# One sync queue with 256 KB transfers, late loads per batch and spread out, and masks ahead of weight casts in a fused attention and feed-forward kernel

## The chip, the cores and the metric

The kernel runs on one core of one Trainium2 chip. The metric is the device time of one execution in microseconds (us); smaller is better. Besides the times there is one profiled execution of each kernel, with a trace of every instruction. The profile names the engines PE (TensorE matmuls), PEld (TensorE weight loads), DVE (VectorE), ACT (ScalarE), POOL (GpSimd) and SP (SyncE). SPq, ACTq and POOLq are the instruction queues from which an engine issues DMAs. "L383" is line 383 of that kernel's source.

## The reference

The first half is linear attention with a decay per head, in blocks along the sequence; the second half is a feed-forward layer with a sigmoid-approximated gelu. There are 4 batches, 8 heads, 768 tokens and a head dimension of 64; the feed-forward layer goes from 512 to 2048 and back.

```python
for b in range(nb):                       # blocks along the sequence (block = 64)
    qb, kb, vb = (q[:, :, sl], k[:, :, sl], v[:, :, sl])
    intra = einsum('bhic,bhjc->bhij', qb, kb) * Dmask     # causal mask with powers of lam
    intra = einsum('bhij,bhjd->bhid', intra, vb)
    inter = einsum('bhid,bhde->bhie', qb * lam_pow, kv_state)
    out[:, :, sl] = intra + inter
    kv_state = lam_block * kv_state + einsum('bhsd,bhse->bhde', kb_dec, vb)
x = out.transpose(0, 2, 1, 3).reshape(B * S, H * D)       # 3072 x 512
h = x @ w_in                                              # 512 -> 2048
g = h * (1 / (1 + exp(-1.702 * h)))
result = g @ w_out                                        # 2048 -> 512
```

## The kernel before

The 768 tokens of each batch are worked through in six "waves" (w = 0 to 5) of 512 columns. Waves 0 and 1 are made of small "units" (one batch and one pair of heads), for a quick start. Waves 2 to 5 are "full" waves of 128 tokens of all four batches. The feed-forward matmuls of wave w stand between the attention work of wave w + 1, so TensorE always has feed-forward work to do as long as the attention work next in its program is ready. TensorE takes its instructions in order. One that waits for data holds up everything behind it, as the wait of 4.75 us shown below does with the feed-forward matmuls that follow it.

All fp32 inputs land in a ring of SBUF buffers. A function per load is put on a list, and `pump()` issues the loads in order as the ring has room. Loads of late waves are put on that list by the schedule itself, at given points. In the kernel before, these late loads (w >= 3) are issued from GpSimd; all others are issued from SyncE:

```python
LATE = 3
...
def load_unit(w, nm, bl, p):              # one unit of one input: 128 KB
    def go(x):
        nc.sync.dma_start(
            out=x.rearrange("s (h c) -> s h c", h=2),
            in_=SRC[nm][2 * w + bl, 2 * p : 2 * p + 2, 0 : 2 * P, :].rearrange("h (q j) d -> q h (j d)", j=2))
        ...
def load_pair(w, nm, p):                  # a pair of heads of all batches: two DMAs of 128 KB
    def go(x):
        x = x.rearrange("s (b h d) -> s b h d", h=2, d=D)
        for h in range(2):
            (nc.sync if w < LATE else nc.gpsimd).dma_start(
                out=x[:, :, h, :],
                in_=SRC[nm][:, 2 * p + h, w * P : (w + 1) * P, :].rearrange("b s d -> s b d"))
        ...
```

A full wave casts and scales k and q on VectorE and then turns them around with a DMA transpose on SyncE's queue. The scores on TensorE need the transposed tile `kq`. The attention result is turned in the same way, from `xs` to `xT`, for the feed-forward layer:

```python
def p_cast(w, p):
    ...
    nc.sync.dma_start_transpose(out=kq_of[w, p].rearrange("p i b s -> p (i b) s"),
                                in_=kqs.rearrange("p i b h d -> p (i b h d)"))
def p_score(w, p):                        # TensorE, waits for kq
    ...
def p_out(w, p):
    ...
    nc.scalar.copy(xs.rearrange("s b h d -> s h b d"), o)
    nc.sync.dma_start_transpose(out=xT(w)[:, p], in_=xs.rearrange("p b h d -> p (b h d)"))
```

The start works through the eight units of wave 0 as a pipeline: unit i is cast and transposed on TensorE while unit i - 1 gets its scores and its state, and unit i - 2 its output:

```python
for i in range(N + 2):
    u, u1, u2 = ...                       # units i, i - 1, i - 2
    if u:
        fill(FILL1); u_turn(0, *u)        # TensorE transposes of the casts
    if u2:
        u_inter(0, *u2)
    if u:
        u_turn_copy(0, *u, nc.scalar)
    if u2:
        u_out(0, *u2)
    if i == N:
        for u_ in ROWS[:2]:
            cast_w("in", *u_, nc.vector)  # w_in casts, ahead of the last mask
    if u1:
        u_score(0, *u1); u_kv0(0, *u1)
        u_mask(0, *u1)                    # VectorE
        u_kv0_copy(0, *u1)                # two ScalarE instructions
    pump()
    ...
```

## Time and profile before

| what | before |
|---|---|
| time, median of 3 runs | 232.38 us (231.28 to 233.66) |
| the profiled execution | 239.61 us, span 237.9 us, mean granted clock 0.971 (a slow run) |
| TensorE busy | 214.9 us, 90% of the span |
| DMA queues | SyncE's 30.42 MB, GpSimd's 9.44 MB |

The profiled execution is some 7 us longer than the median, so sizes read from it must be scaled with care.

The page of the kernel before cuts the span into 40 slices (5.9 us each). A digit is the share of the slice in tenths that TensorE was busy, and that the TensorE clock was granted:

```profile
PE   7887998999999297999595999999999999999993
PEclk9997999999999679999999799999999999999999
```

TensorE is full except at the start and between slices 14 and 22 (some 77 to 130 us), and there the clock falls too. The table of busy time by window of the kernel before shows the middle closer. The columns are the window, its length, then busy time and (in brackets) number of instructions of PE, PEld, DVE, ACT and POOL, then the granted clock, the DMA share and GB/s:

```profile
60.00:72.00 12.00, 12.00 (x131) 6.91 (x128) 3.95 (x11) 7.19 (x19) 4.84 (x8) 1.00 1.18 232
72.00:84.00 12.00, 7.25 (x71) 5.12 (x69) 7.13 (x19) 4.04 (x11) 8.88 (x13) 0.79 1.03 158
84.00:96.00 12.00, 10.38 (x115) 5.31 (x113) 7.22 (x14) 1.17 (x2) 9.44 (x14) 0.92 1.13 193
108.00:130.00 22.00, 16.03 (x153) 8.10 (x152) 9.42 (x19) 8.39 (x15) 12.43 (x19) 1.00 1.12 152
130.00:170.00 40.00, 40.00 (x288) 19.00 (x286) 20.75 (x42) 13.07 (x22) 17.63 (x24) 0.96 0.70 153
```

What TensorE waited for is in the list of waits of the kernel before (total us, times, longest us):

```profile
PE ps_s L383 <- DMA kq<-kqs: 12.3, 5, 4.7
PE ps_o L358 <- DVE sm L301: 0.9, 1, 0.9
```

The scores (`ps_s`) wait 12.3 us for the DMA transposes. That transposes are slow here, and not late in the schedule, is in the view of the tile `kq`: its DMA line gives the issue time on SyncE's queue in ns (min/median/max), its last line the time to landing:

```profile
L374 SPq DMA_TRANSPOSE kq<-kqs x16: 1232/1358/4887, 73.1 to 181.6; - x16
DMA to landing us min/median/max: 3.1/6.1/15.1
```

By themselves (after 147 us) these transposes land in 3.1 to 3.8 us; between 73 and 130 us they take 8.5 to 15.1 us. In SyncE's timeline four of them occupy the queue for 13.79 us:

```profile
73.08 13.79 SPq L374 DMA_TRANSPOSE kq<-kqs  x4
```

TensorE's timeline of the kernel before shows what such a wait costs (start us, duration us, engine, line, operation, in brackets the idle time before it and its cause):

```profile
81.61 0.61 PE L383 MATMUL ps_s<-kq 64*128 64x128 bf16 x8 [4.75 <-DMA kq<-kqs]
82.15 0.61 PE L398 MATMUL ps_kv<-v_sb,kqs 128*128 128x128 bf16 x4
82.55 1.91 PE L470 MATMUL ps_out<-w_out,g_sb 128*128 128x512 bf16 x4
...
129.16 0.40 PE L383 MATMUL ps_s<-kq 64*128 64x128 bf16 x8 [2.53 <-DMA kq<-kqs]
130.07 4.44 PE L470 MATMUL ps_out<-w_out,g_sb 128*128 128x512 bf16 x12
```

The wait is paid twice. After 4.75 us of idle the four big matmuls take 1.91 us, where four take about 1.03 us at full clock; after 2.53 us of idle twelve take 4.44 instead of 2.75 us. After waits of 1.6 and 1.7 us, elsewhere in the same timeline, the clock stayed whole.

The same view of the start of the kernel before:

```profile
21.12 0.43 PE L358 MATMUL ps_o<-sm,v_sb 64*64 64x128 bf16 x8 [0.92 <-DVE sm L301]
21.48 3.56 PE L439 MATMUL ps_h<-xT,w_in 128*128 128x512 bf16 x9
```

A mask (`sm`) came 0.92 us late, because it stood behind a weight cast on VectorE, and the first nine feed-forward matmuls then ran at half clock.

### The profile page before, as it was taken

How to read it: one execution, taken by the hardware profiler on the slowest of the kernel's cores; microseconds unless marked ns; L12 is line 12 of the kernel's file. 1: busy time of each engine (PE TensorE's matmuls, PEld its weight loads, DVE VectorE, ACT ScalarE, POOL GpSimd, SP SyncE). 2: the span in 40 equal slices, each digit the busy share in tenths (PEclk: the TensorE clock that was granted, in tenths of full speed). 3: DMA queues.
4: the chain of work that ended last, by engine and by line, in shares of the span. 5: the costliest groups of instructions: out<-in, count | busy, mean ns of one | idle time of the engine just before them, and what ended most of it. 6: DMA issues, size and time to landing. Idle time of an engine off the chain costs nothing.

```text
span 237.9 us, 4615 instructions
## 1 busy us (share of the span) xinstructions
PE 214.9 (90%) x1772; PEld 109.5 (46%) x1772; DVE 106.8 (45%) x233; ACT 99.6 (42%) x211; POOL 81.8 (34%) x131
## 2 busy tenths in 40 slices
PE   7887998999999297999595999999999999999993
PEld 3453444665467144443253444454444454444453
DVE  3566455693238265555363228567153451200121
ACT  5795657655747000126340105661026630166100
POOL 7650051032339577598572996200000000000000
PEclk9997999999999679999999799999999999999999
DMA  5889989999999999999998999912329014110012
GB/s 143 248 209 350 362 227 329 363 257 218 229 230 204 120 195 196 225 247 172 180 138 149 199 229 272 163 25 47 112 88 176 15 32 133 46 44 0 35 56 88
DMA packets 63286, 40.16 MB, mean 169 GB/s; under 512 B 41376, under 2 KB 53920, under 8 KB 63264
## 3 DMA queue, kind: packets, MB, share of 16 engines
q1 hardware_dynamic: 59664, 30.42, 52.4%
q0 software_dynamic: 3456, 9.44, 21.2%
q8 instruction: 14, 0.23, 0.4%
q14 instruction: 8, 0.07, 0.1%
q10 hardware_dynamic: 144, 0.00, 0.0%
HBM read 27.27 MB, written 6.29 MB: 141 GB/s over the span
## 4 chain that ended last, share of the span: by engine, by line
PE 64%; DMA 27%; SPq 4%; ACT 1%; DVE 1%; issue 1%; POOL 0%; ACTq 0%
PE ps_out L470 30%; PE ps_h L439 24%; DMA kq<-kqs 13%; DMA xT<-xs 5%; DMA ring<-in_moe_w_in_dram 5%; SPq L90 4%; DMA ring<-in_q_dram 2%; PE ps_s L383 2%; PE ps_o L420 2%; DMA ring<-in_k_dram 2%; PE ps_out L486 1%; PE ps_t L275 1%; PE ps_kv L398 1%; PE ps_o L413 1%; PE ps_kv L336 1%; PE ps_s L296 1%
## 5 line engine op out<-in xcount | busy, mean ns | idle before, releaser
L439 PE MATMUL ps_h<-xT,w_in 128*128 128x512 bf16 (+1 forms) x448 | 89.6, 353 | 0.9 <-ACT g_sb L445 0.5
L470 PE MATMUL ps_out<-w_out,g_sb 128*128 128x512 bf16 x368 | 86.4, 390 | 0.0
L445 ACT ACTIVATE g_sb<-ps_h 128x512 bf16<-128x512 f32 (+1 forms) x112 | 59.6, 536 | 60.9 <-PE ps_h L439 59.5
L439 PEld LDWEIGHTS <-w_in 128*128 128x128 bf16 x448 | 42.6, 99 | 40.1 <-issue 3.6
L470 PEld LDWEIGHTS <-g_sb 128*128 128x128 bf16 x368 | 35.7, 100 | 41.1 <-issue 3.8
L390 DVE SCALAR_TENSOR_TENSOR sm<-ps_s,inv_pow,mask 128x512 bf16<-128x512 f32 x32 | 22.6, 747 | 37.1 <-PE ps_s L383 37.1
L477 DVE COPY o_sb<-ps_out 128x512 f32<-128x512 f32 x19 | 13.1, 691 | 54.3 <-PE ps_out L470 51.5
L423 ACT CAST xs<-ps_o 128x512 bf16<-128x512 f32 x16 | 9.4, 585 | 44.8 <-PE ps_o L420 29.2
L258 POOL TENSOR_TENSOR kqs<-ring,kq_pow 128x256 bf16<-128x256 f32 x16 | 10.2, 637 | 34.7 <-DMA ring<-in_q_dram 33.9
L101 POOL DMA_DIRECT2D ring<-in_q_dram x24 | 17.8, 747 | 5.6 <-DMA ring<-in_k_dram 4.5
L101 POOL DMA_DIRECT2D ring<-in_v_dram x24 | 17.9, 749 | 3.6 <-DMA ring<-in_q_dram 2.0
L101 POOL DMA_DIRECT2D ring<-in_k_dram x24 | 18.0, 756 | 0.7 <-DMA ring<-in_v_dram 0.6
L372 POOL CAST v_sb<-ring 128x512 bf16<-128x512 f32 x16 | 10.3, 662 | 23.0 <-DMA ring<-in_v_dram 20.3
L383 PE MATMUL ps_s<-kq 64*128 64x128 bf16 x128 | 6.6, 224 | 12.3 <-DMA kq<-kqs 12.3
L301 DVE TENSOR_TENSOR sm<-ps_s,mask 128x512 bf16<-128x512 f32 x16 | 11.0, 689 | 10.5 <-PE ps_s L296 6.1
L383 PEld LDWEIGHTS <-kq 64*128 64x128 bf16 x128 | 3.7, 96 | 19.6 <-DMA kq<-kqs 15.8
L370 DVE TENSOR_SCALAR kqs<-ring,k_pow 128x256 bf16<-128x256 f32 x32 | 11.7, 406 | 0.2
L370 DVE TENSOR_SCALAR kqs<-ring,q_pow 128x256 bf16<-128x256 f32 x32 | 11.8, 408 | 0.0
L402 DVE SCALAR_TENSOR_TENSOR kv<-kv,blk,ps_kv 64x256 bf16<-64x256 bf16 x24 | 11.4, 475 | 0.2
L258 DVE TENSOR_TENSOR kqs<-ring,kq_pow 128x256 bf16<-128x256 f32 x16 | 8.3, 529 | 5.2 <-ACT kq_pow L204 2.7
L250 PE MATMUL ps_f<-zeros 128*128 128x512 bf16 x28 | 8.7, 438 | 1.3 <-DVE zeros L173 1.3
L283 ACT COPY kq<-ps_t 128x512 bf16<-128x512 bf16 x12 | 7.0, 585 | 5.8 <-PE ps_t L275 5.4
(66 smaller groups left out, 135.2 us busy)
## 6 DMA issues: line engine op xcount, KB each, us to landing
ring<-in_moe_w_in_dram SPq DMA_DIRECT2D x16, 256.0 KB, 6.5
ring<-in_moe_w_out_dram SPq DMA_DIRECT2D x16, 256.0 KB, 5.3
out_dram<-o_sb SPq DMA_DIRECT2D x15, 256.0 KB, 2.2
ring<-in_k_dram SPq DMA_DIRECT2D x24, 128.0 KB, 3.6
ring<-in_q_dram SPq DMA_DIRECT2D x24, 128.0 KB, 3.6
ring<-in_v_dram SPq DMA_DIRECT2D x24, 128.0 KB, 3.7
ring<-in_k_dram POOLq DMA_DIRECT2D x24, 128.0 KB, 7.0
ring<-in_q_dram POOLq DMA_DIRECT2D x24, 128.0 KB, 6.7
```

What stands on the lines that cost most here:

```text
L101: (nc.sync if w < LATE else nc.gpsimd).dma_start(out=x[:, :, h, :], in_=SRC[nm][:, 2 * p + h, w * P : (w + 1) * P, :].rearrange("b s d -> ...
L258: eng.tensor_tensor(kqs_of[w, p][:, bl, i].rearrange("s j h d -> s h j d"), read(w, "kq"[i], bl, p), tab, op=MUL)
L301: nc.vector.tensor_tensor(sm.rearrange("s h j t -> s h (j t)"), s_ps.pop((w, bl, p))[:, :, 0 : 2 * P], mask2.to_broadcast([P, 2, 2 * P]), ...
L370: nc.vector.tensor_scalar(kqs[:, i, :, h, :], x[:, :, h, :], scalar1=(k_pow, q_pow)[i][:, 2 * p + h : 2 * p + h + 1], scalar2=None, op0=MUL)
L372: nc.gpsimd.tensor_copy(v_sb[w % 2][:, p], read(w, "v", p))
L383: nc.tensor.matmul(s[:, h, b, :], t[hd(h), 0, b, :], t[hd(h), 1, b, :], start=True, stop=True)
L390: nc.vector.scalar_tensor_tensor(sm[:, h], s[:, h], inv_pow[:, 2 * p + h : 2 * p + h + 1], mask.to_broadcast([P, B, P]), op0=MUL, op1=MUL)
L402: nc.vector.scalar_tensor_tensor(new[hd(h), p], old[hd(h), p], blk2[hd(h), p : p + 1], t[hd(h), :, hd(h)], op0=MUL, op1=ADD)
L439: nc.tensor.matmul(t[:, bs[0] * P : bs[1] * P], w_in_sb[fc // CW][:, kc, (fc % CW) * P : (fc % CW + 1) * P], xT(w)[:, kc, bs[0] : bs[1], : ...
L445: nc.scalar.activation(g_tile(w)[:, fc, c], h_ps.pop((w, fc))[:, c], GELU)
L470: nc.tensor.matmul(t, g_of[w][:, fc, g * P : (g + 1) * P], w_out_sb[j][:, fc % CW, :], start=(fc == 0), stop=(fc == FFC - 1))
L477: nc.vector.tensor_copy(o, t)
```

## The change

The intent has four parts. All loads go on SyncE's queue, so that no second queue runs beside the transposes. Transfers become 256 KB: units are loaded in twos, and the full waves per batch with all eight heads. The late loads are spread out one by one in the schedule. In the start, the last mask goes ahead of the weight casts, and every second pair of kv_bd copies goes from ScalarE to one VectorE multiplication with a block-diagonal table, for which the kv matmuls become twice as wide. The diff, cut to its core:

```diff
-    def load_unit(w, nm, bl, p):
+    def load_units(w, nm, bl, p, n=2):
...
-                in_=SRC[nm][2 * w + bl, 2 * p : 2 * p + 2, 0 : 2 * P, :].rearrange("h (q j) d -> q h (j d)", j=2))
+                in_=SRC[nm][2 * w + bl, 2 * p : 2 * (p + n), 0 : 2 * P, :].rearrange("h (q j) d -> q h (j d)", j=2))
...
-    def load_pair(w, nm, p):
+    def load_batch(w, nm, b):
         def go(x):
-            x = x.rearrange("s (b h d) -> s b h d", h=2, d=D)
-            for h in range(2):
-                (nc.sync if w < LATE else nc.gpsimd).dma_start(
-                    out=x[:, :, h, :],
-                    in_=SRC[nm][:, 2 * p + h, w * P : (w + 1) * P, :].rearrange("b s d -> s b d"))
+            if b == 0:
+                loaded[w, nm] = x.rearrange("s (b p h d) -> s b p h d", b=B, h=2, d=D)
+            nc.sync.dma_start(out=loaded[w, nm][:, b].rearrange("s p h d -> s (p h) d"),
+                              in_=SRC[nm][b, :, w * P : (w + 1) * P, :].rearrange("h s d -> s h d"))
...
-    UNITS = [(bl, p) for p in range(NP) for bl in range(2)]
+    UNITS = [(bl, p) for g in range(2) for bl in range(2) for p in (2 * g, 2 * g + 1)]
+    LOADS0 = [(0, 0, 1), (0, 1, 1), (1, 0, 2), (0, 2, 2), (1, 2, 2)]
...
+    for bl, p, n in LOADS0:
+        for nm in "kqv":
+            load_units(0, nm, bl, p, n)
...
-    def u_kv0_copy(w, bl, p):
+    def u_kv0_copy(w, bl, p, eng):
...
+        else:
+            eng.tensor_tensor(kv_bd[:, p, 2 * w + bl].rearrange("s h d -> s (h d)"), t,
+                              blk_bd[:, p].rearrange("s h d -> s (h d)"), op=MUL)
...
+        blk_bd = const.tile([P, NP, 2, D], f32)
+        nc.gpsimd.memset(blk_bd, 0.0)
...
-            if i == N:
-                for u_ in ROWS[:2]:
-                    cast_w("in", *u_, nc.vector)
             if u1:
                 u_score(0, *u1)
                 u_kv0(0, *u1)
+                if i == N:
+                    cast_w("in", *ROWS[0], nc.vector)
                 u_mask(0, *u1)
-                u_kv0_copy(0, *u1)
+                u_kv0_copy(0, *u1, nc.vector if i % 2 else nc.scalar)
+                if i == N:
+                    cast_w("in", *ROWS[1], nc.vector)
...
         def load_spread(t0, w, step):
-            for p in range(NP):
-                for i, nm in enumerate("kqv"):
-                    at(t0 + step * (3 * p + i), load_pair, w, nm, p)
+            for i, nm in enumerate("kqv"):
+                for b in range(B):
+                    at(t0 + step * (B * i + b), load_batch, w, nm, b)
```

More of the change, by code (lines that the diff above doesn't have):

```diff
@@ L82, with load_batches @@
     NR = 26
-    LATE = 3
     ring = const.tile([P, 2 * NR, W // 2], f32, name="ring")
     head, used, where, coming = [0], set(), {}, []
-    def load_unit(w, nm, bl, p):
+    def load_units(w, nm, bl, p, n=2):
         def go(x):
             nc.sync.dma_start(
-                out=x.rearrange("s (h c) -> s h c", h=2),
-                in_=SRC[nm][2 * w + bl, 2 * p : 2 * p + 2, 0 : 2 * P, :].rearrange("h (q j) d -> q h (j d)", j=2))
-            loaded[w, nm, bl, p] = x.rearrange("s (h j d) -> s h j d", h=2, j=2)
-        coming.append((1, (w, nm, bl, p), go))
-    def load_pair(w, nm, p):
-        def go(x):
-            x = x.rearrange("s (b h d) -> s b h d", h=2, d=D)
-            for h in range(2):
-                (nc.sync if w < LATE else nc.gpsimd).dma_start(
-                    out=x[:, :, h, :],
-                    in_=SRC[nm][:, 2 * p + h, w * P : (w + 1) * P, :].rearrange("b s d -> s b d"))
-            loaded[w, nm, p] = x
-        coming.append((2, (w, nm, p), go))
+                out=x.rearrange("s (h c) -> s h c", h=2 * n),
+                in_=SRC[nm][2 * w + bl, 2 * p : 2 * (p + n), 0 : 2 * P, :].rearrange("h (q j) d -> q h (j d)", j=2))
+            for i in range(n):
+                loaded[w, nm, bl, p + i] = x.rearrange("s (n h j d) -> s n h j d", n=n, h=2, j=2)[:, i]
+        coming.append((n, [(w, nm, bl, p + i) for i in range(n)], 1, go))
+    def load_batch(w, nm, b):
+        def go(x):
+            if b == 0:
+                loaded[w, nm] = x.rearrange("s (b p h d) -> s b p h d", b=B, h=2, d=D)
+            nc.sync.dma_start(out=loaded[w, nm][:, b].rearrange("s p h d -> s (p h) d"),
+                              in_=SRC[nm][b, :, w * P : (w + 1) * P, :].rearrange("h s d -> s h d"))
+        coming.append((2 * B if b == 0 else 0, [(w, nm)] if b == 0 else [], NP, go))
+    def load_batches(w):
+        for nm in "kqv":
+            for b in range(B):
+                load_batch(w, nm, b)
     def load_w(kind, j, r):
@@ L115, in go @@
             loaded[kind, j, r] = x
-        coming.append((2, (kind, j, r), go))
+        coming.append((2, [(kind, j, r)], 1, go))
     def pump():
         while coming:
-            n, key, go = coming[0]
-            i = (head[0] + (n - 1) * (head[0] % 2)) % (2 * NR)
+            n, keys, reads, go = coming[0]
+            i = (head[0] + (head[0] % 2 if n > 1 else 0)) % (2 * NR)
+            if n == 0:
+                coming.pop(0)
+                go(None)
+                continue
+            if i + n > 2 * NR:
+                i = 0
             if any(c in used for c in range(i, i + n)):
                 break
+            m = n // max(1, len(keys))
+            for a, key in enumerate(keys):
+                where[key] = [range(i + a * m, i + (a + 1) * m), reads]
             used.update(range(i, i + n))
-            where[key] = (i, n)
             head[0] = i + n
@@ L131, in read @@
     def read(*key):
-        i, n = where.pop(key)
-        used.difference_update(range(i, i + n))
-        return loaded.pop(key)
-    def load_full(w):
-        for p in range(NP):
-            for nm in "kqv":
-                load_pair(w, nm, p)
+        where[key][1] -= 1
+        if where[key][1] == 0:
+            used.difference_update(where.pop(key)[0])
+            return loaded.pop(key)
+        return loaded[key]
     def cast_w(kind, j, r, eng):
@@ L149 @@
     nc.scalar.dma_start(out=lam_p, in_=bass.AP(tensor=lam.tensor, offset=lam.offset, ap=[[0, P], [1, H]]))
-    UNITS = [(bl, p) for p in range(NP) for bl in range(2)]
+    UNITS = [(bl, p) for g in range(2) for bl in range(2) for p in (2 * g, 2 * g + 1)]
+    LOADS0 = [(0, 0, 1), (0, 1, 1), (1, 0, 2), (0, 2, 2), (1, 2, 2)]
     A_UNITS, B_UNITS = [(0, p) for p in range(NP)], [(1, p) for p in range(NP)]
-    for i, u in enumerate(UNITS):
-        load_unit(0, "k", *u)
-        load_unit(0, "q", *u)
-        if i:
-            load_unit(0, "v", *UNITS[i - 1])
-    load_unit(0, "v", *UNITS[-1])
+    for bl, p, n in LOADS0:
+        for nm in "kqv":
+            load_units(0, nm, bl, p, n)
     for u in ROWS:
         load_w("in", *u)
-    for u in A_UNITS:
-        for nm in "kqv":
-            load_unit(1, nm, *u)
-    for u in ROWS:
-        load_w("out", *u)
-    for u in B_UNITS:
-        for nm in "kqv":
-            load_unit(1, nm, *u)
-    load_full(2)
+    for bl in range(2):
+        for p in (0, 2):
+            for nm in "kqv":
+                load_units(1, nm, bl, p)
+        if bl == 0:
+            for u in ROWS:
+                load_w("out", *u)
+    load_batches(2)
     pump()
@@ L314, in u_kv0 @@
         if w == 0:
-            t = ps.tile([P, W], f32, tag="t", bufs=1, name="ps_kv")[:, 0:D]
+            t = ps.tile([P, W], f32, tag="t", bufs=1, name="ps_kv")[:, 0:P]
         else:
-            t = o_cur[0][:, 0, P : P + D]
+            t = o_cur[0][:, 0, P : 2 * P]
         kv_ps[w, bl, p] = t
@@ L320, in u_kv0 @@
             for j in range(2):
-                nc.tensor.matmul(t[hd(h), :], kqs_of[w, p][hd(0), bl, 0, j, h], v_sb[w % 2][hd(0), p, 2 * bl + j, h],
+                nc.tensor.matmul(t[hd(h), :], kqs_of[w, p][hd(0), bl, 0, j, h],
+                                 v_sb[w % 2][hd(0), p, 2 * bl + j].rearrange("s h d -> s (h d)"),
                                  start=(j == 0), stop=True, skip_group_check=True)
-    def u_kv0_copy(w, bl, p):
+    def u_kv0_copy(w, bl, p, eng):
         t = kv_ps.pop((w, bl, p))
-        for h in range(2):
-            nc.scalar.activation(kv_bd[hd(h), p, 2 * w + bl, h, :], t[hd(h), :], COPY, scale=blk2[hd(h), p : p + 1])
+        if eng is nc.scalar:
+            for h in range(2):
+                nc.scalar.activation(kv_bd[hd(h), p, 2 * w + bl, h, :], t[hd(h), hd(h)], COPY,
+                                     scale=blk2[hd(h), p : p + 1])
+        else:
+            eng.tensor_tensor(kv_bd[:, p, 2 * w + bl].rearrange("s h d -> s (h d)"), t,
+                              blk_bd[:, p].rearrange("s h d -> s (h d)"), op=MUL)
     def u_state(w, p):
@@ L367, in p_cast @@
         for i in range(2):
-            x = read(w, "kq"[i], p)
+            x = read(w, "kq"[i])
             for h in range(2):
-                nc.vector.tensor_scalar(kqs[:, i, :, h, :], x[:, :, h, :],
+                nc.vector.tensor_scalar(kqs[:, i, :, h, :], x[:, :, p, h, :],
                                         scalar1=(k_pow, q_pow)[i][:, 2 * p + h : 2 * p + h + 1], scalar2=None, op0=MUL)
-        nc.gpsimd.tensor_copy(v_sb[w % 2][:, p], read(w, "v", p))
+        nc.gpsimd.tensor_copy(v_sb[w % 2][:, p], read(w, "v")[:, :, p])
         kq_of[w, p] = work.tile([P, 2, B, P], bf16, tag=f"kq{p}", name="kq")
@@ L502 @@
         nc.gpsimd.memset(kv_bd, 0.0)
+        blk_bd = const.tile([P, NP, 2, D], f32)
+        nc.gpsimd.memset(blk_bd, 0.0)
+        for h in range(2):
+            nc.gpsimd.tensor_copy(blk_bd[hd(h), :, h, :],
+                                  blk2[hd(h)].rearrange("s (p d) -> s p d", d=1).to_broadcast([64, NP, D]))
         N = len(UNITS)
@@ L582, in units1 @@
                 if 0 < i <= n:
-                    at(h, u_kv0_copy, 1, *units[i - 1])
+                    at(h, u_kv0_copy, 1, *units[i - 1], nc.scalar)
         def states(t0, w, step):
@@ L603, in load_spread @@
         def load_spread(t0, w, step):
-            for p in range(NP):
-                for i, nm in enumerate("kqv"):
-                    at(t0 + step * (3 * p + i), load_pair, w, nm, p)
+            for i, nm in enumerate("kqv"):
+                for b in range(B):
+                    at(t0 + step * (B * i + b), load_batch, w, nm, b)
         HA, HB = (0, 2), (2, 4)
```

## The prediction

> **What bounds the kernel now.** TensorE: in the table of stages (busy time by window) it has no gap from 130 us to the tail, and the page gives it 90% of the 237.9 us span. Two places are left to win.
>
> 1. Waves 2 and 3, 72 to 130 us. The list of waits gives "PE ps_s <- DMA kq<-kqs" 12.3 us: TensorE waits for the DMA transposes. They take 10 to 15 us to landing here (the view of tile kq), but 3.3 to 3.6 us after 147 us, when no loads run. Beside them run the GpSimd-queue loads. The DMA view of 66 to 135 us shows that queue with packets of 2.7 KB (7.25 MB in 2,657), the hardware queue, which carries the transposes, with 360 bytes (5.53 MB in 15,210). The Trainium skill ("DMA: Bandwidth & Descriptors", Queues, rings and completion order) says that each DMA engine goes round-robin between queues, a packet at a time; the slowed transposes agree. I count idle of 4.75, 1.6, 0.3, 1.7, 1.7 and 2.5 us = 12.6 us. After the 4.75 and the 2.5 us the granted clock is 0.50 for a while (8 matmuls take 3.5 us, 12 take 4.4, instead of 1.7 and 2.6): 3.7 us more. About 16 us in all.
> 2. The start. The sync queue issues one 128 KB load per 0.51 us (255 GB/s) until 14 us; units follow at about 1.6 us, with ScalarE busy 7.1 of 8 us. At 20 us TensorE waits 0.9 us for a mask that stands behind a weight cast on VectorE; then the clock is 0.50 from 21 to 24.5 us, and the first gelu waits.
>
> **What the change does.**
> - All loads go in order with the transposes on one queue. A transpose waits at most behind one or two 256 KB loads: an estimate from the 225 GB/s of 256-byte rows at 54 to 66 us is 1.2 us each, so 4 to 6 us to landing, against a lead of some 8 us in the schedule. Of 16 us I expect 14 back. GpSimd loses 54 us of DMA work, which in itself is worth nothing.
> - Start: 256 KB per issue lifts the issue limit; 512-byte rows then run at some 285 GB/s (seen 48 to 54 us), so wave 0 lands about 2 us earlier, and w_in behind it. Half of the kv_bd copies (0.63 us per unit) leave ScalarE. The mask precedes the second cast, and the clock may not fall. Against it: GpSimd makes blk_bd before its first cast, about 0.9 us, and kv matmuls are twice as wide (about 1 us in all). Net 3 us; wave 1's first units 0.5 us.
> - Whole k and q batches must land before p_cast; the schedule has them in time.
>
> **Sum.** 237.9 - 14 - 3.5 = 220.4 us span, plus the 1.7 us by which the run exceeds the span: 222. The profiled run is a slow one (239.6 against the median 232.4), so against the median the gain is about 11 us. I predict **221 us**, 217 to 226.5. Faster by over 2%: 0.94; within 2%: 0.05; slower: 0.01.
>
> **What shows it.** Right: kq transposes land in 4 to 6 us everywhere, "PE ps_s <- DMA kq" under 2 us, clock 1.0 from 72 to 135 us, first gelu at 21 to 22 us instead of 24.6. Wrong: transposes still over 8 us, or TensorE waiting for casts that wait for a whole batch.
>
> **What would make it wrong.** A sync queue that stands at a transpose or store and holds back loads behind it; 256-byte rows slower than 225 GB/s; the blk_bd setup delaying every unit.

## The result

| | before | after |
|---|---|---|
| time, median | 233.02 us (4 runs, 231.28 to 235.44) | 220.85 us (4 runs, 220.24 to 220.90) |
| ratio of fast runs | | 0.9495, 95% interval 0.9431 to 0.9559 |
| profiled span | 237.9 us (slow run) | 218.7 us (fast run) |
| TensorE busy | 214.9 us, 90% | 207.8 us, 95% |

A ratio here is the mean time of one kernel's fast runs over the mean of the other's of the same rounds, so it is not quite the ratio of the medians. The kernel became 5% faster. The slices of the page after show TensorE full from the ninth slice on (5.5 us each), and the clock whole everywhere:

```profile
PE   7887999899999999999999999999999999999993
PEclk9999999999999999999999999999999999999999
```

The windows of the kernel after, cut at the same times as before:

```profile
72.00:84.00 12.00, 11.89 (x143) 7.37 (x141) 10.32 (x24) 3.80 (x9) 0.00 (x0) 1.00 1.10 193
84.00:96.00 12.00, 11.95 (x82) 5.77 (x80) 6.57 (x16) 2.80 (x5) 0.00 (x0) 1.00 1.09 209
108.00:130.00 22.00, 21.75 (x160) 10.67 (x162) 11.74 (x24) 5.53 (x10) 2.67 (x4) 1.00 0.89 185
```

In the stretches between 72 and 130 us that lost time before, TensorE now idles for 0.25 us at most. The wait "PE ps_s <- DMA kq" is gone from the list of waits of the kernel after. Its two largest entries are now these, of the filling matmuls at the very start and of the units before 66 us:

```profile
PE ps_f L255 <- DVE zeros L178: 1.3, 1, 1.3
PE ps_o L360 <- ACT kv_bd L335: 1.1, 4, 0.4
```

The view of the tile `kq` after:

```profile
L385 SPq DMA_TRANSPOSE kq<-kqs x16: 1232/1264/1797, 69.1 to 163.5; - x16
DMA to landing us min/median/max: 3.1/3.5/5.2
```

The longest transpose lands in 5.2 us instead of 15.1, and the longest issue is 1.8 us instead of 4.9. The start of the kernel after, in TensorE's timeline:

```profile
21.06 0.23 PE L360 MATMUL ps_o<-kq,kv_bd 128*128 128x128 bf16 x1 [0.39 <-ACT kv_bd L335]
21.22 0.31 PE L369 MATMUL ps_o<-sm,v_sb 64*64 64x128 bf16 x8
21.46 2.12 PE L450 MATMUL ps_h<-xT,w_in 128*128 128x512 bf16 x9
```

The nine feed-forward matmuls begin at the same time as before (21.46 against 21.48 us), but take 2.12 us instead of 3.56. The first gelu starts at 23.37 instead of 24.64 us. The feed-forward work of wave 1's second half starts at 66.32 instead of 68.31 us. So 2.0 us of the difference in span (19.2 us) were won by then, and the other 17 us come from the middle. The profiled before was a slow run, and against the medians the gain is 12 us.

### The profile page after: what moved, and what is told of

Same layout as the page of the kernel before. It is cut to its first block, busy times and chain, and to the rows that moved or that the text cites. A ratio compares the mean times of both kernels' runs of the same rounds, so it can differ in the third digit from the quotient of the medians.

```text
span 218.7 us, 4482 instructions
## 1 busy us (share of the span) xinstructions
PE 207.8 (95%) x1745; PEld 108.6 (50%) x1772; DVE 105.2 (48%) x237; ACT 97.4 (45%) x203; POOL 30.3 (14%) x62
## 4 chain that ended last, share of the span: by engine, by line
PE 84%; DVE 4%; ACT 4%; DMA 2%; issue 2%; SPq 1%; POOL 1%
PE ps_h L450 35%; PE ps_out L481 35%; PE ps_o L431 2%; PE ps_s L394 2%; DMA ring<-in_q_dram 2%; DVE w_out L150 2%; PE ps_out L497 2%; SPq L89 1%; ACT kv_bd L335 1%; PE ps_kv L409 1%; PE ps_o L369 1%; PE ps_o L424 1%; PE ps_t L280 1%; PE ps_o L360 1%; PE ps_s L301 1%
## 5 line engine op out<-in xcount | busy, mean ns | idle before, releaser
L450 PE MATMUL ps_h<-xT,w_in 128*128 128x512 bf16 (+1 forms) x438 | 87.1, 348 | 1.3 <-ACT g_sb L456 0.7
L481 PE MATMUL ps_out<-w_out,g_sb 128*128 128x512 bf16 x354 | 80.8, 379 | 0.8 <-issue 0.3
L481 PEld LDWEIGHTS <-g_sb 128*128 128x128 bf16 x368 | 34.8, 98 | 38.9
L381 DVE TENSOR_SCALAR kqs<-ring,q_pow 128x256 bf16<-128x256 f32 x32 | 11.1, 390 | 0.0
L263 DVE TENSOR_TENSOR kqs<-ring,kq_pow 128x256 bf16<-128x256 f32 x16 | 7.5, 474 | 5.5 <-DMA ring<-in_k_dram 3.0
L350 DVE TENSOR_TENSOR kv<-kv_bd,ps_kv 64x128 bf16<-64x128 bf16 x16 | 4.6, 286 | 8.2 <-PE ps_kv L347 7.9
L371 ACT CAST xT<-ps_o 128x256 bf16<-128x256 f32 x16 | 6.0, 373 | 3.6 <-PE ps_o L369 3.5
L280 PEld LDWEIGHTS <-kqs 128*128 128x128 bf16 x64 | 4.7, 98 | 5.7 <-DVE kqs L263 1.9
L280 PE MATMUL ps_t<-ident,kqs 128*128 128x128 bf16 x64 | 6.4, 220 | 1.0 <-POOL kqs L263 0.7
L150 DVE CAST w_out<-ring 128x512 bf16<-128x512 f32 x16 | 7.1, 498 | 0.1
```

The source lines that it names most:

```text
L150: eng.tensor_copy((w_in_sb if kind == "in" else w_out_sb)[j][:, r, :], read(kind, j, r))
L263: eng.tensor_tensor(kqs_of[w, p][:, bl, i].rearrange("s j h d -> s h j d"), read(w, "kq"[i], bl, p), tab, op=MUL)
L280: nc.tensor.transpose(t_ps[w, bl, p][:, i, j, :], kqs_of[w, p][:, bl, i, j].rearrange("s h d -> s (h d)"), ident)
L381: nc.vector.tensor_scalar(kqs[:, i, :, h, :], x[:, :, p, h, :], scalar1=(k_pow, q_pow)[i][:, 2 * p + h : 2 * p + h + 1], scalar2=None, op0 ...
L450: nc.tensor.matmul(t[:, bs[0] * P : bs[1] * P], w_in_sb[fc // CW][:, kc, (fc % CW) * P : (fc % CW + 1) * P], xT(w)[:, kc, bs[0] : bs[1], : ...
L481: nc.tensor.matmul(t, g_of[w][:, fc, g * P : (g + 1) * P], w_out_sb[j][:, fc % CW, :], start=(fc == 0), stop=(fc == FFC - 1))
```

## The experiments

Theory A (the prediction's): the transposes are slowed by loads on GpSimd's queue that share the DMA engines with them, and the loads' move to the transposes' own queue is what the middle won; the start won by earlier data. Rivals: it is the order and spread of the loads, or the transfer size, whatever the queue; and for the start, the mask order or the split of the copies. There were twelve runs of eleven kernels, on three chips, each beside the kernel before (233.74, 234.25 and 234.35 us in the median). The kernel after was not run again. It was run at another time. All numbers after a label are medians with their range; where only one run was made, it is said.

### 1. The queue alone, taken back: q_pool

```diff
-            nc.sync.dma_start(out=loaded[w, nm][:, b]...
+            (nc.sync if w < 3 else nc.gpsimd).dma_start(out=loaded[w, nm][:, b]...
```

> The changed kernel with one thing undone: the per-batch loads of waves 3 to 5 are issued from GpSimd again, same sizes, same places in the program. Theory A (the gain of the middle stage comes from having the loads on the transposes' own queue): the stalls come back, kq transposes land in 8 to 15 us beside the loads, TensorE waits for them 8 us or more in all, and the time is 229 to 233 us. Theory B (it comes from the larger, per-batch, spread-out transfers, whatever the queue): at most 223 us and transposes under 6 us.

The three timed runs took 245.2, 246.16 and 246.43 us; the ratio to before is 1.0569 (1.0471 to 1.0667). A fourth execution, the profiled one, took 541 us with its matmuls slow throughout. It is an anomaly that is set aside, and its trace is not used. The kernel was therefore profiled once more, with no change to it:

> The same kernel as q_pool, for a profile in its ordinary state, since that of q_pool fell into an execution of 541 us whose matmuls ran slowly throughout. About 246 us. Theory A: kq transposes land in 8 to 15 us beside the loads of the GpSimd queue, TensorE waits for them, the clock falls. Rival: the transposes land as after the change (3 to 5 us), and TensorE waits for casts whose whole k and q batches come late from a GpSimd that stands in waits.

This single run took 244.37 us. The list of waits of this run:

```profile
PE ps_h L450 <- DMA xT<-xs: 9.5, 2, 5.0
PE ps_s L394 <- DMA kq<-kqs: 7.7, 2, 6.7
```

The landing line of `kq` in this run:

```profile
DMA to landing us min/median/max: 3.1/4.1/14.0
```

The transposes of waves 2 and 3, which run beside the loads of later waves, land in 7.1 to 14.0 us and in 4.7 to 7.6 us. With everything else of the change in place, the loads' queue alone costs 25 us, twice the whole gain. A rival that does without the queue falls with this run.

### 2. The queue alone, given to the kernel before: before_sync

```diff
-    LATE = 3
+    LATE = NW
```

> The kernel before with one thing done: the loads of waves 3 to 5 go from GpSimd to the sync queue, still 128 KB each and per pair of heads. Theory A: nearly the whole middle-stage gain, transposes land in 3 to 6 us, 222 to 224 us (only the start's part of some 2 us is missing). Theory B: it stays above 228 us.

It took 226.81 us (226.44 to 227.76), ratio 0.9753 (0.9678 to 0.9829). One constant is worth 7 of the 13 us between the before of this call and the kernel after; counted by the means of fast runs alone, each kernel beside its own before, it is 5.7 of 11.7 us. So it is about half. The transposes land as in the kernel after (3.2/3.5/5.3 us), yet the expectation of theory A, 222 to 224 us, was missed by about 3 us. TensorE's waits in this run:

```profile
PE ps_h L439 <- DMA xT<-xs: 2.8, 1, 2.8
PE ps_s L383 <- DMA kq<-kqs: 1.5, 1, 1.5
```

These waits come from transposes that are issued late. From 71 to 130 us SyncE's queue is never free for long: every 256 KB of loads takes two instructions and 1.1 us, where the changed kernel takes one and 0.57 us. The transpose that TensorE waits for at 98 us was issued at 95.31 us, behind such pairs and stores. So the transfer size matters in the middle too, through the issuing queue's time.

### 3. Another queue that is not GpSimd's: q_act

```diff
+            (nc.sync if w < 3 else nc.scalar).dma_start(out=loaded[w, nm][:, b]...
```

> The changed kernel with the loads of waves 3 to 5 issued from ScalarE, whose queue is another hardware queue than the transposes', so that its packets are small like theirs. Theory A in its narrow form (packets of a foreign queue take turns with the transposes', and it is the 2.7 KB packet that starves them): the transposes are slowed only about twofold, 5 to 8 us. If any foreign queue did as much harm as GpSimd's they would take 8 to 15 us. ScalarE itself loses some 20 us to issuing and may stand in waits, so the time can rise to 222 to 232 us for that reason; the verdict is read from the landing times of kq.

It took 221.92 us (221.34 to 222.22), ratio 0.9529, about 1 us more than the kernel after. The landing line of `kq` in this run:

```profile
DMA to landing us min/median/max: 3.1/4.5/7.3
```

A second queue does stretch the transposes, but to 7.3 and not to 14 us, and the schedule's lead hides most of it: the stalls are 0.39 and 0.57 us.

### 4. Order and spread on the one queue: burst

```diff
-        load_spread(e + 4, 3, 1.8)
+        load_spread(e + 4, 3, 0.1)
...
-                load_spread(e + 4, w + 2, 2.4)
+                load_spread(e + 4, w + 2, 0.1)
```

> The changed kernel with the loads of a wave put in one clump (step 0.1 in place of 1.8 and 2.4), so that ten 256 KB loads stand in the same queue between the second and the third transpose of a wave. If the order in the one queue is what protects a transpose, the third and fourth kq transpose of waves 2 to 4 land late, 8 to 14 us after issue or issued late, and TensorE waits for them: 225 to 232 us. If one queue alone suffices, however the loads stand in it: 221 us.

It took 245.81 us (245.34 to 246.12), ratio 1.0562 (1.0486 to 1.0638), as slow as with GpSimd's queue, but for another reason. The transposes land quickly (3.1/3.6/4.9 us). SyncE's timeline of this run shows when they are issued:

```profile
69.42 3.04 SPq L385 DMA_TRANSPOSE kq<-kqs  x2
72.52 4.41 SPq L101 DMA_DIRECT2D ring<-in_k_dram  x4
76.97 4.84 SPq L101 DMA_DIRECT2D ring<-in_q_dram  x4
81.86 2.33 SPq L101 DMA_DIRECT2D ring<-in_v_dram  x2
84.30 2.31 SPq L385 DMA_TRANSPOSE kq<-kqs  x1
```

The third transpose stands behind ten loads, at over 1.1 us of queue time each, and TensorE idles 7.88 us for it until 89.04 us. A load of 256 KB takes 0.57 us of this queue where it stands alone; 256 KB in 1.15 us are 228 GB/s, about what rows of 256 bytes gave elsewhere, so in a block the queue runs at the pace of the data. Why is not shown. The built program has eight DMA semaphores, and a DMA uses the one of the eighth DMA before it; but for each of the ten loads that eighth DMA had landed at least 4 us before the load was issued (for the load at 73.98 us, which took 1.74 us of the queue, at 66.95 us), so a wait for it is not the cause. One queue is thus not enough: the spread keeps loads from standing in a block ahead of a transpose.

### 5. What about GpSimd's queue slows the transposes: act_burst and act_burst_2k

The prediction explained the slow transposes by packet size: GpSimd's queue moved packets of 2.7 KB (7.25 MB in 2,657), the hardware queue of 360 bytes. The Trainium skill ("DMA: Bandwidth & Descriptors", SWDGE vs HWDGE vs iDMA) gives at most 4,096 bytes as the preferred packet, with which 2.7 KB agrees: in the trace's table of packets all data packets of GpSimd's queue between 66 and 135 us have 4,096 bytes, and 4-byte ones pull the mean down. To test it, the clump of loads was put on ScalarE's queue, once as it is and once with rows of 2 KB. The second kernel reads w_out in place of k, q and v (relative error 0.72). Its output is wrong, which doesn't matter for the time.

```diff
             # act_burst: burst's load_spread, and for w >= 3
+            nc.scalar.dma_start(out=loaded[w, nm][:, b]..., in_=<as before>)
             # act_burst_2k: the same, but
+            nc.scalar.dma_start(out=loaded[w, nm][:, b].rearrange("s p h d -> s (p h d)"),
+                                in_=moe_w_out[r0 : r0 + P, :])
```

> Late loads from ScalarE's queue and in a clump, so that twelve 256 KB loads of 256-byte rows certainly run beside the kq transposes (in q_act they were paced by the gelus). If small packets of a foreign hardware queue share the engines evenly, the transposes land in 5 to 8 us; if any other queue starves them, in 8 to 15 us. The time may be long, as ScalarE stands in its own DMA waits: 225 to 250 us.

> As act_burst, but each late load reads 128 rows of 2 KB of w_out in place of 1,024 rows of 256 bytes of q, k or v; same bytes, same place in the ring. The result is wrong on purpose. If it is the size of the foreign packets that starves the transposes (2.7 KB on the GpSimd queue), they land later than in act_burst while such loads run, 8 to 15 us; if that is peculiar to the GpSimd queue, they land as in act_burst or sooner.

Their times, 264.19 and 259.42 us (one run each), say nothing of the question: ScalarE stands at the DMAs' waits and its gelus come late (37.5 and 31.6 us of TensorE's waits). The packets were as wanted, as the queue lines between 66 and 135 us show. The first line is of act_burst:

```profile
q10 hardware_dynamic: 24960, 6.29, 56.2%
```

The same line of act_burst_2k, with the same bytes in a seventh of the packets:

```profile
q10 hardware_dynamic: 3456, 6.29, 31.0%
```

So the packets are 252 bytes in one and 1.8 KB in the other. The transposes beside the loads of waves 3 and 4 land in 6.4, 6.1, 8.3 and 5.9, 6.4, 8.1 us with the small packets, and in 6.1, 6.7, 8.5 and 4.9, 7.7, 9.2 us with the large ones; beside those of wave 5 it is 5.4, 5.6, 7.7 against 4.9, 8.5, 10.5 us. Over all 16 transposes min, median and max are 3.1/5.5/8.3 and 3.1/4.9/10.5 us. Of the nine beside loads, six land later and three sooner with the large packets, and their mean goes from 6.7 to 7.4 us. So in one run each, packets seven times as large bring about a tenth, and come nowhere near the factor of 3 to 4 between the 10 to 15 us of the prediction and its 3.3 to 3.6 us. The test has limits: packets of 2 KB are half of GpSimd's, and whether the unit that the profile counts as a packet is the one between which a DMA engine switches queues is not shown. What makes GpSimd's queue worse than ScalarE's (up to 15.1 against 8.3 to 10.5 us) stays open.

### 6. The start: st_loads, st_mask, st_kv

Each takes one part of the start's change back.

```diff
 # st_loads: wave 0 in 128 KB loads
-    LOADS0 = [(0, 0, 1), (0, 1, 1), (1, 0, 2), (0, 2, 2), (1, 2, 2)]
+    LOADS0 = [(bl, p, 1) for bl, p in UNITS]
 # st_mask: both casts ahead of u_score, as before
+            if i == N:
+                for u_ in ROWS[:2]:
+                    cast_w("in", *u_, nc.vector)
 # st_kv: no blk_bd, all copies on ScalarE
-                u_kv0_copy(0, *u1, nc.vector if i % 2 else nc.scalar)
+                u_kv0_copy(0, *u1, nc.scalar)
```

> The changed kernel with its first loads (wave 0) cut to 128 KB each as before, in the changed order of units. The prediction held that the 0.51 us per issue of such loads paces the units of the start, and that 256 KB loads win about 2 us: then 222 to 223 us. The rival, formed from the trace after the change, is that the units are paced at 1.58 us by a loop of one buffer each (inter, scores and kv on TensorE, then the mask or the kv_bd copy, then the next inter) whatever the loads do: then 220.3 to 221.2 us, and the last xT copy still ends near 22 us.

> The changed kernel with the first two weight casts ahead of the last masks on VectorE again. If this order is what kept the clock up at 21 us, the wait of about 0.9 us and the half clock come back in most executions, the first gelu is again near 24.6 us, and the time is 221.8 to 222.6 us. If the clock was saved by something else: 220.5 to 221.2 us.

> The changed kernel with all kv_bd copies on ScalarE again and without the table blk_bd that GpSimd makes for the VectorE copies. If taking half the copies off ScalarE speeds up the units (the prediction), this costs 1 us or more: 222 us. If the loop paces them and the table only delays the first unit by 1.2 us (rival), this gains about 1 us: 219.5 to 220.3 us, with the first transposes at 5.7 us instead of 6.9.

| kernel | median of 6 runs, us | range |
|---|---|---|
| st_loads | 223.91 | 223.54 to 226.71 |
| st_mask | 220.49 | 220.18 to 221.58 |
| st_kv | 221.0 | 220.79 to 222.23 |

Only the size of the loads counts, with 3.1 us against the 220.85 of the kernel after, and not where it was expected. The window table of st_loads:

```profile
16.00:21.00 5.00, 3.79 (x81) 2.14 (x80) 3.40 (x9) 3.23 (x9) 1.28 (x3) 1.00 0.86 248
25.00:32.00 7.00, 4.99 (x25) 2.07 (x22) 3.84 (x9) 3.80 (x7) 0.00 (x0) 1.00 1.11 346
32.00:40.00 8.00, 6.55 (x88) 3.42 (x87) 4.98 (x10) 4.11 (x10) 4.23 (x8) 1.00 1.09 361
```

The same windows of the kernel after:

```profile
16.00:21.00 5.00, 3.34 (x73) 2.00 (x72) 3.41 (x9) 3.48 (x9) 0.83 (x2) 1.00 0.99 360
25.00:32.00 7.00, 6.95 (x37) 3.27 (x36) 2.83 (x7) 4.78 (x8) 2.33 (x5) 1.00 1.13 313
32.00:40.00 8.00, 7.40 (x109) 4.03 (x108) 4.97 (x11) 6.46 (x16) 1.91 (x4) 1.00 1.05 385
```

In wave 0's units st_loads is no slower: its first gelu is even earlier (22.93 against 23.37 us). It loses between 25 and 40 us, where TensorE waits 2.01, 0.85 and 0.60 us for wave 1's casts, whose first starts at 31.30 instead of 28.28 us. Until 13 us its queue issued one load of 128 KB per 0.51 us without a break, so w_in was issued from 13.11 instead of 10.58 us (from 16 to 21 us 248 against 360 GB/s were moved), and wave 1's data came behind it.

The mask order is worth nothing once the loads come early. In the kernel before, the w_in casts on VectorE waited 6.0 us in all for their DMA, in st_mask 1.2 us; with 256 KB loads the first tiles are already there, so in st_mask the two casts don't hold the mask up, and the mask starts at 19.72 us. In st_loads, with late data and the new order, the clock stayed whole as well. Only with both undone (before and before_sync) did it fall at 21 us. Either part was enough in these profiles, of one execution each; and four executions of the kernel before with a clock of 0.998 or more leave no room for a fall, so the old start does not always bring it.

The split of the copies is worth nothing either, and why is not shown. st_kv's first transposes come 0.4 us earlier (6.47 against 6.89 us), not 1.2, and the missing table is not needed to explain it: they stand behind 14 filling matmuls, which took 5.38 against 5.80 us because the clock became whole at 5.72 instead of 6.55 us, and st_mask and reorder, which make the table, have them at 6.56 and 6.53 us. The units of st_kv follow at about 1.6 us as well, and the gelu table is loaded at 22.53 instead of 21.97 us.

### 7. Could the start be better: reorder and best

The units follow at about 1.6 us with all versions so far. A guess was a loop between TensorE and ScalarE, to be broken by putting the scores of unit i - 1 ahead of the output of unit i - 2 on TensorE. The kernel best adds a later making of the table, behind the first unit's casts.

```diff
+            if u1:
+                u_score(0, *u1); u_kv0(0, *u1)
             if u:
                 u_turn_copy(0, *u, nc.scalar)
             if u2:
+                u_inter(0, *u2)
                 u_out(0, *u2)
-            if u1:
-                u_score(0, *u1); u_kv0(0, *u1)
```

> The changed kernel with one reordering in the start: on TensorE the scores and kv of a unit come before the inter and out of the unit ahead of it, so that the kv_bd copy has a whole step to finish. If the loop through kv_bd paces the start (rival), the units go at 1.3 to 1.4 us instead of 1.58, the first gelu comes 1 to 2 us earlier, and the time is 218.8 to 219.8 us. If loads or ScalarE's busy time pace them: no change, 220.8 us.

> The reordering of the run reorder, and besides the table blk_bd is filled by GpSimd after the first unit's casts instead of before them. If the loop and the table's delay of 1.2 us both stood on the start's critical path: 217.8 to 218.8 us, the first gelu near 21 us. If the reordering alone counts: as reorder, 219 to 219.8 us. If neither: 220.8 us.

The kernel reorder took 221.06 us (220.74 to 222.2), and best 221.53 us (220.85 to 223.15; ratio 0.9502). Neither beats the kernel after, and the guess of 218.8 to 219.8 us fell. In the trace of reorder the units still follow at 1.5 to 1.8 us: the kv matmuls now wait for their one PSUM bank, which a kv_bd copy frees that stands behind the xT copy on ScalarE. The loop was moved, not broken. What paces the units stays open.

## Why the prediction was right

The time was right: 221 us were predicted and 220.85 came, and the kernel is faster by over 2%. That it fits to 0.2 us is luck in part. Against the slow profiled run 14 us had been counted for the middle and 3.5 for the start, and 17 and 2.0 came, so that two errors offset each other; and the step from there to "about 11 us" against the median was not worked out (12 came).

- **The middle was right in place and in size.** The waits of 12.6 us and the half clock behind them are gone, the transposes land in 3.1 to 5.2 us (4 to 6 had been predicted), and the clock is 1.00 from 72 to 170 us. That the loads' queue is the cause is shown from both sides: taken back alone it costs 25 us (q_pool), given alone it wins 6 to 7 us (before_sync).
- **The mechanism behind it was only half right.** The round robin of queues by packets, taken from the Trainium skill ("DMA: Bandwidth & Descriptors", Queues, rings and completion order), is compatible with q_act, where a second queue stretches the transposes from 3.5 to 4.5 us in the median. But the size of the packets, which the prediction put at the centre, was worth about a tenth where seven times larger ones were tried (act_burst_2k), and ScalarE's queue did less harm than GpSimd's with small and large ones. What it is about GpSimd's queue stays open.
- **One thing was missed: the time of the issuing queue.** The prediction named "a sync queue that stands at a transpose or store and holds back loads" as a danger, but not the opposite, loads holding back transposes. The runs show that this is the other half of the change: burst loses 25 us to it, and before_sync keeps 4.3 us of such waits in its profile.
- **The start was about right in size and wrong in its path.** Net 3 us had been predicted for it; the profiles show 2.0 us won by 66 us, and st_loads puts 3.1 us on the load size. But the first gelu came at 23.37 and not at 21 to 22 us. The units didn't speed up: they follow at about 1.6 us before and after, and the first transposes start 1.3 us later (6.89 against 5.60 us). Most of that is not the change's doing: the clock became whole at 6.55 instead of 3.95 us, at times that lie between 3.95 and 7.21 us over all start experiments, and the 14 filling matmuls ahead of the transposes took 5.80 instead of 4.51 us. GpSimd's making of the table (memset 0.52 us and copies 0.85 us) ran beside them; in st_mask TensorE waited 0.55 us for the cast behind it. The kv_bd copies and the mask order, to which the prediction gave a share, are worth nothing by themselves. What pays are, in the profiled executions, the whole clock at 21.5 us (1.4 us) and the earlier w_in and wave 1.
- **The clock.** The Trainium skill ("TensorE: Matmul & The Clock Gate", What's actually happening) says that the clock is halved after an idle window of about 3.4 us that runs freely, and released again by activity. In the trace's clock record of the kernel before, the stretches of half clock that begin at 21.02, 79.04 and 130.24 us last 3.41, 6.83 and 3.41 us, whole multiples of one length. But the length of a single wait does not decide. The 3.41 us ahead of each of these three falls, with the busy time of TensorE (the second number) at 1.68, 1.23 and 1.08 us:

```profile
17.61:21.02 3.41, 1.68 (x25) 0.86 (x26) 1.88 (x5) 1.65 (x6) 0.00 (x0) 1.00 0.97 303
75.63:79.04 3.41, 1.23 (x12) 0.86 (x9) 2.41 (x7) 1.49 (x4) 3.41 (x6) 1.00 1.14 95
126.83:130.24 3.41, 1.08 (x29) 0.97 (x30) 0.64 (x1) 0.00 (x0) 1.03 (x2) 1.00 1.13 205
```

In before_sync the clock fell at 21.42 us, after the first of these stretches, and not after the other two, although a wait of 2.80 us (95.23 to 98.03 us) lies across them:

```profile
18.01:21.42 3.41, 1.70 (x33) 1.01 (x33) 2.34 (x5) 1.82 (x6) 0.00 (x0) 1.00 0.95 313
93.10:96.51 3.41, 2.13 (x10) 0.88 (x9) 1.80 (x6) 0.00 (x0) 0.04 (x1) 1.00 0.90 212
96.51:99.92 3.41, 1.89 (x9) 0.87 (x9) 2.13 (x9) 1.20 (x2) 0.00 (x0) 1.00 0.75 176
```

So the clock fell after stretches in which TensorE was busy for half or less (32 to 50%), and stayed whole after 55 and 62%. A wait of 2.53 us was enough in one place, and one of 2.80 us, divided between two stretches, was not in another. The border is not sharp, or not seen in busy time alone: in the kernel before 50% (116.59 to 120.00 us) and in q_pool_look 41% (77.71 to 81.12 us) brought no fall.

The parts don't add up neatly: 6 to 7 us for the queue, 3.1 us for the first wave's loads and up to 4.3 us for fewer issues in the middle make 13 to 14, where the medians give 12 to 13. Loads that come early in the start also change what the middle has to wait for, and the kernel before scatters by several microseconds.

## What to carry to other kernels

Where a DMA transpose stands on the critical path, look at its time from issue to landing in each stage: if it grows to several times its lone value, look for loads on another queue beside it; in this kernel GpSimd's did most harm. Moving those loads to the transposes' queue helped here only with few, large loads spread between the transposes, because that queue issues in order and its issue time is then shared. When idle gaps of 2.5 us or more on TensorE go, look at the granted clock whether half-clocked matmuls stood behind them, and count those as part of the gain; but look at several executions, since the same kernel also ran without them.

## What the Trainium skill lacked or had wrong

- "DMA: Bandwidth & Descriptors", Issuing engines are not separate DMA queues, says that issuing from several engines saves only the time to initiate DMAs. Here the same loads gave 246 us from GpSimd, 222 from ScalarE and 221 from SyncE; transposes beside them took up to 14.0 (15.1 in the kernel before), 7.3 and 5.2 us to land. The page gives no effect of one queue's loads on another's latency.
- The same section calls the time to initiate a DMA "usually small relative to the DMA itself". On SyncE it was 1.2 to 1.4 us for a transpose that lands in 3.1 to 3.5 us, about 0.57 us for a load of 256 KB and as much for one of 128 KB; in burst ten loads ahead of a transpose held it for 11.7 us (72.5 to 84.2 us). The page's DMA Transpose section gives neither the issue nor the landing time, and elsewhere the page has only an effective bandwidth and, for other shapes, cycles of the sequencer.
- The same page's section on bandwidth, from measurements of DMAs issued by GpSimd, advises 1 MiB or more per DMA for three quarters of the peak. Here, in a stream of transfers of 256 KB on one queue, up to 394 GB/s were reached with 2 KB rows (21 to 25 us before), 300 GB/s with 512-byte rows (8 to 13 us after) and 213 GB/s with 256-byte rows (49 to 61 us after). No page has a measured rate for such streams on this chip.
- "TensorE: Matmul & The Clock Gate" gives an idle window of about 3.4 us for the fall of the clock, and does not say how much activity still counts as idle. Here the clock fell after stretches of 3.41 us with 32 to 50% busy time and stayed whole after some with 41 to 62%, so one wait of 2.53 us was followed by half clock (12 matmuls in 4.44 us) and one of 2.80 us was not.
